# One load of raw inputs split into four pieces, each with a tile of its own

## The chip, the cores and the metric

The kernel runs on one NeuronCore of a Trainium2 chip. The core has five engines with a queue of instructions each: TensorE (PE, matrix products; PEld is its weight loading), VectorE (DVE), ScalarE (ACT), GpSimd (POOL) and SyncE (SP), which in this kernel issues every DMA. Each engine works through its queue in order, and an instruction whose input is not there yet holds up all that stand behind it. The metric is the time of one execution on the device, in microseconds (us); lower is better.

## The reference

Six arrays r, k, v, w, a, b of shape 4 x 8 x 768 x 40 (batch, heads, time steps, features) drive a recurrence with a 40 x 40 state per batch and head. Its output goes through two dense layers with different gates:

```
for t in range(768):                      # for each of 4 x 8 batch-heads
    y[t]  = r[t] @ state
    Sa    = state @ a[t]
    state = state * w[t][None, :] - outer(Sa, b[t]) + outer(v[t], k[t])
x = y as 3072 tokens x 320
h = x @ w_in;   x = (h * sigmoid(h)) @ w_out       # first layer, d_ff 2048
h = x @ w_in2;  out = (h - tanh(h)) @ w_out2       # second layer
```

## The kernel before

The 768 steps are cut into 12 chunks of 64, and each chunk into two halves (`hf`) of 16 batch-heads. In a chunk the recurrence is rewritten as matrix products with running products of w. Work on a chunk c goes through these steps:

- `load_raw` (L196): one DMA brings the half's packed inputs from the DRAM tensor `pk` into the tile `raw`, 120 partitions x 2311 float32: 384 columns of a, 768 of k and b, 384 of r, 384 of v, and 391 of w, in this order. `raw` has one buffer. The second half of chunk 0 is an exception and goes into a spare `LR` buffer.
- `prep` (L210): DVE runs a forward scan over w (L226), a reciprocal (L227), two small writes of `HL` (L228, L229) and a scaling of a (L231), then a backward scan over w (L232) and a scaling of k and b (L235). POOL scales r and v (L194, called at L238) and subtracts (L191, L241) to get the low float16 parts of numbers that ACT rounds to float16 (L236, L237, L239, L240). The result `HL` (one buffer) goes to an `LR` tile (five buffers) in 12 SBUF-to-SBUF DMAs (L252).
- `p1`, `p2`: products of the features (L267, L287), their masked copies `mK` (L275) and `bP` (L279, L280).
- `sol_in`, 31 times `sol_step`, `sol_out`: a triangular solve on DVE (L302, L311, L313, L323, L324), then two merges on PE (L331, L345).
- `ch_x`, `ch_u`, `ch_s`, `ch_y`, `ch_m`: the chain over chunks, mostly PE with short evictions; the state goes on in `MT` and `M`, copied by DMA (L447, L448, L477, L478). The `LR` buffer of a half is free after them. In this stretch DVE also evicts `lows` (L387, L475), `Md` (L437) and `Sm` (L407).
- `x_t1`, `x_t2`, with the decay factors `pf` loaded at L482 and scanned at L487; then the first dense layer for the chunk's 256 tokens: `mm_h` (L567, L568), `act1`, `mm_o` (L589 to L591), `out1`.

Beside these the weights of both layers are converted (`conv_wi`, `conv_wo`: loads of `cr` at L515, work at L523 to L526). The second layer is a stage of its own after everything else.

The table `SC` gives each step of each chunk a time in an abstract unit; the steps are traced in the order of these times, and a scheduler then fixes each engine's order with a model of durations and of buffers that come free. So a change of a tile or a load can move instructions of all engines. For `load_raw` the time is that of `raw`, kept behind the `prep` of the half before.

Of the kernel before, what the change touches and what calls it, by code (L numbers as in the profile page):

```python
# [7 lines left out]
F32 = mybir.dt.float32  # L8
# [10 lines left out]
C = 64  # L19
# [7 lines left out]
RAWN = 5 * 384 + 391  # L27
# [4 lines left out]
S_R = 2.0 ** 10  # L32
# [15 lines left out]
def _poly():  # L48
# [21 lines left out]
    raw=(-10.4107, -10.0452),  # L70
# [13 lines left out]
    x=(-0.5853, 0.3603, 0.8835, 1.3808),  # L84
    xe=0.02,
    u=(0.6994, 1.3329, 1.3307, 2.0705),
# [13 lines left out]
    o=4.7895,  # L100
# [5 lines left out]
def build(tc, pk, tv, wf, w1i, w1o, w2i, w2o, out, nch=NCH, dbg=None):  # L106
    nc = tc.nc
    PE, ACT, DVE, POOL, SP = nc.tensor, nc.scalar, nc.vector, nc.gpsimd, nc.sync
# [13 lines left out]
    at_p = ph1.enter_context(tc.tile_pool(name="at", bufs=1))  # L122
# [56 lines left out]
    def planes(HL):  # L179
        return [HL[:, :, o:o + n] for o, n in ((0, LW), (LW, 2 * C), (RW, LW), (RW + LW, 2 * C))]  # L180
# [5 lines left out]
    P_t, raw_t, L_t, R_t, KBt_t, VU_t, MT_t, M_t, U_t = {}, {}, {}, {}, {}, {}, {}, {}, {}  # L186
# [3 lines left out]
    def psub(out, a, b):  # L190
        POOL.tensor_tensor(out, a, b, ALU.subtract)  # L191

    def pscale(out, a, sc):
        POOL.tensor_scalar(out, a, sc, 0.0, ALU.mult, ALU.add)  # L194

    def load_raw(c, hf):  # L196
        if c == 0 and hf == 1:
            t = lr_slot().rearrange("p u n -> p (u n)").bitcast(F32)[0:120, 0:RAWN]
        else:
            t = at_p.tile([120, RAWN], F32, tag="raw", name="raw", bufs=1)  # L200
        SP.dma_start(out=t, in_=pk[c, hf])
        raw_t[c, hf] = t

    def load_v(c, hf):
        t = VU_s[hf]
# [2 lines left out]
        VU_t[c, hf] = t  # L208

    def prep(c, hf):  # L210
        raw = raw_t.pop((c, hf))
        hl = HL
        if c == 0 and hf == 1:
            hl = lr_slot().rearrange("p u n -> p (u n)")[0:120, 0:12 * RW].rearrange("p (j n) -> p j n", j=6)
            DVE.memset(planes(hl)[0][:, :, 3 * C:LW], 0.0)
        ll, rh, lh, rl = planes(hl)
        k0, v0 = (0, 2 * C) if c % 2 == 0 else (C, 0)

        def sl(i, n):
            return raw[:, i:i + 6 * n].rearrange("p (j t) -> p j t", t=n)  # L220

        av, kb, rv, vv, w = sl(0, C), sl(384, 2 * C), sl(1152, C), sl(1536, C), raw[:, 1920:RAWN]

        pt = at_p.tile([120, 392], F32, tag="pq", name="pq", bufs=1)
        pq = pt[:, 0:390].rearrange("p (j t) -> p j t", t=65)
        DVE.tensor_tensor_scan(pt[:, 0:390], w[:, 0:390], d1a.rearrange("p j t -> p (j t)"), 0.0, ALU.mult, ALU.add)  # L226
        DVE.reciprocal(out=d1b[:, 65:391:65], in_=pt[:, 64:390:65])  # L227
        DVE.tensor_scalar(lh[:, :, 3 * C:3 * C + 1], pq[:, :, C:C + 1], S_P * S_KB / P_INIT, None, ALU.mult)  # L228
        DVE.scalar_tensor_tensor(out=lh[:, :, 3 * C + 1:LW], in0=pq[:, :, C:C + 1], scalar=S_P * S_KB / P_INIT,  # L229
                                 in1=lh[:, :, 3 * C:3 * C + 1], op0=ALU.mult, op1=ALU.subtract)  # L230
        DVE.scalar_tensor_tensor(out=av, in0=av, scalar=-S_A * S_KB, in1=pq[:, :, 0:C], op0=ALU.mult, op1=ALU.mult)  # L231
        DVE.tensor_tensor_scan(pt[:, 2:391][:, ::-1], w[:, 2:391][:, ::-1], d1b[:, 2:391][:, ::-1], 0.0, ALU.mult, ALU.add)  # L232
        pi = pt[:, 2:392].rearrange("p (j t) -> p j t", t=65)[:, :, 0:C]
        kbv = kb.rearrange("p j (q t) -> p j q t", q=2)
        DVE.tensor_tensor(kbv, kbv, pi.unsqueeze(2).to_broadcast([120, 6, 2, C]), ALU.mult)  # L235
        ACT.activation(out=lh[:, :, k0:k0 + 2 * C], in_=kb, func=AF.Copy)  # L236
        ACT.activation(out=rh[:, :, 0:C], in_=av, func=AF.Copy)  # L237
        pscale(raw[:, 1152:1920], raw[:, 1152:1920], S_R)  # L238
        ACT.activation(out=rh[:, :, C:2 * C], in_=rv, func=AF.Copy)  # L239
        ACT.activation(out=lh[:, :, v0:v0 + C], in_=vv, func=AF.Copy)  # L240
        (DVE if c == 0 else POOL).tensor_tensor(ll[:, :, k0:k0 + 2 * C], kb, lh[:, :, k0:k0 + 2 * C], ALU.subtract)  # L241
        psub(rl[:, :, 0:C], av, rh[:, :, 0:C])
        psub(ll[:, :, v0:v0 + C], vv, lh[:, :, v0:v0 + C])
        psub(rl[:, :, C:2 * C], rv, rh[:, :, C:2 * C])
        if c == 0:
            gates["pool"] = nc.cur_bb.bb.instructions[-1]
        LR = lr_slot()
        for i in range(3):
            n = 6 if i < 2 else 4
            src, dst = hl[i * 40:i * 40 + 40, 0:n], LR[:, 6 * i:6 * i + n]  # L250
            for pl, s0, d0, w in ((0, RW, 0, LW), (0, LW, LW, 2 * C), (1, RW, 0, RW), (2, 0, 0, RW)):
                SP.dma_start(out=dst[pl * 40:pl * 40 + 40, :, d0:d0 + w], in_=src[:, :, s0:s0 + w])  # L252
        LR = LR[0:120].rearrange("p (u j) n -> p u j n", u=2)
        L, R = LR[:, :, :, 0:LW], LR[:, :, :, LW:RW]
        if c == 0:
            gates["sp"] = nc.cur_bb.bb.instructions[-1]
        p63 = at_p.tile([40, 2, 8, 1], F32, tag="p63", name="p63", bufs=5)
        POOL.tensor_tensor(p63, L[0:40, :, :, 3 * C:3 * C + 1], L[0:40, :, :, 3 * C + 1:LW], ALU.add)
        L_t[c, hf], R_t[c, hf], P_t[c, hf] = L, R, p63
# [36 lines left out]
    def lr_slot():  # L296
        return at_p.tile([128, 16, RW], F16, tag="LR", name="LR", bufs=5)
# [357 lines left out]
    for c in range(nch):  # L655
        T0 = 8.0 * c
        T1 = T0 + (SC["d"][c] if c < len(SC["d"]) else 0)
        for hf in range(2):
            when(T1 + SC["raw"][hf], load_raw, c, hf, after=[("prep", c - 1 + hf, 1 - hf)] if c else [])
            when(T1 + SC["prep"][hf], prep, c, hf, after=[("load_raw", c, hf)] + ([("prep", c, 0)] if hf else []))  # L660
            when(T0 + SC["v"][hf], load_v, c, hf, after=[("ch_y", c - 1, 2 * hf), ("ch_y", c - 1, 2 * hf + 1)])
# [15 lines left out]
        for nm, fn, fe in (("x", ch_x, ch_xe), ("u", ch_u, ch_ue), ("s", ch_s, ch_se), ("y", ch_y, ch_ye), ("m", ch_m, ch_me)):  # L677
            for b in range(4):
                hf = b // 2
# [25 lines left out]
    if not dbg:  # L705
        for f in range(NF):
            at(SC["c1"][0] + f * SC["c1"][1], conv_w1, conv_wi, mo, w1i, wih[:, f], f)
            at(SC["c1"][0] + SC["c1"][2] + f * SC["c1"][1], conv_w1, conv_wo, mo, w1o, woh[:, f], f)
            for q in range(2):
                n = 2 * f + q  # L710
# [79 lines left out]
```

## Time and profile before

| what | value |
|---|---|
| median of three runs | 1278.87 us (1276.74 to 1279.15) |
| profiled execution | 1283.47 us, of which 1281.4 us are the profile's span |
| mean granted TensorE clock | 0.932 of full speed |
| busy share of the span | PE 83%, DVE 76%, ACT 64%, POOL 33% |
| raw loads | 23 into `raw`, one into `LR`, 1083.3 KB each |

The span begins with a stretch of some 100 us in which PE has almost nothing to do. From there to about 860 us chunks overlap with the first dense layer. What is left of the first layer runs to about 900 us, the second layer's weights are loaded, and the second layer takes the last 351 us. Times in the rows below are us from the start of the span unless they say ns.

### The profile page before, as it was taken

The numbers are of one execution on the slowest core, as the hardware profiler recorded it, in microseconds if no ns is written. First come the engines' busy times: TensorE is split into PE (matmuls) and PEld (weight loads), VectorE is DVE, ScalarE is ACT, GpSimd is POOL, SyncE is SP. The second block draws the span as 40 slices with busy tenths as digits, with TensorE's granted clock in tenths as the row PEclk, the third lists the DMA queues.
The fourth block names the chain that finished last, engine by engine and source line by source line (L and its number), as shares of the span: only waits on it lengthen the run. The fifth ranks groups of instructions, "written<-read, shape, count | busy, mean of one in ns | idle before, by whom it ended". The sixth has DMA issues, their size and how long they took to land.

```text
span 1281.4 us, 31698 instructions
## 1 busy us (share of the span) xinstructions
PE 1063.9 (83%) x12624; PEld 879.2 (69%) x12624; DVE 971.2 (76%) x1871; ACT 822.5 (64%) x1586; POOL 421.6 (33%) x490
## 2 busy tenths in 40 slices
PE   0006578798889889889888998999999999999997
PEld 0005566677677667767776777888778888888885
DVE  6678998788887868878677787853238788888885
ACT  2456687666767657645545454554259888888886
POOL 5334544434424333423232231010013333333332
PEclk9999759879898979989897998999989999999999
DMA  5565665555656554353424432110701111111100
GB/s 129 144 146 154 173 155 138 146 146 147 159 143 171 141 160 114 101 116 96 108 74 96 108 94 74 31 47 21 216 24 24 24 33 27 33 25 24 24 12 21
DMA packets 154955, 122.36 MB, mean 95 GB/s; under 512 B 89528, under 2 KB 140152, under 8 KB 151928
## 3 DMA queue, kind: packets, MB, share of 16 engines
q1 hardware_dynamic: 154808, 120.35, 36.5%
q8 instruction: 99, 1.62, 0.5%
q14 instruction: 48, 0.39, 0.1%
HBM read 63.59 MB, written 13.89 MB: 60 GB/s over the span
## 4 chain that ended last, share of the span: by engine, by line
PE 22%; issue 18%; DMA 17%; DVE 17%; POOL 9%; SPq 8%; ACT 8%; POOLq 0%; DVEq 0%; ACTq 0%
DMA raw<-pk 8%; POOL gl L191 7%; PE hp L567 7%; SPq L252 5%; DMA LR<-HL 3%; DVE Tl L313 3%; DVE tmp L311 2%; PE o L589 2%; PE o L591 2%; PE o L590 2%; DMA pf<-wf 2%; SPq L632 2%; PE psx L361 2%; PE psu L376 1%; ACT cr L525 1%
## 5 line engine op out<-in xcount | busy, mean ns | idle before, releaser
L567 PE MATMUL hp<-xh,wih 128*128 128x256 f16 x960 | 196.7, 291 | 13.9 <-DVE gl L577 13.7
L567 PE MATMUL hp<-x,w 128*128 128x256 f16 x1344 | 189.5, 273 | 0.0
L191 POOL TENSOR_TENSOR gl<-q,gh 128x512 f16<-128x512 f32 x96 | 111.3, 1159 | 207.8 <-ACT gh L624 207.8
L567 PEld LDWEIGHTS <-wih 128*128 128x128 f16 x1344 | 131.9, 103 | 39.5 <-issue 15.4
L567 PEld LDWEIGHTS <-w 128*128 128x128 f16 x1344 | 131.5, 98 | 22.9
L313 DVE TENSOR_TENSOR Tl<-Tl,tmp 128x126 f32<-128x126 f32 (+22 forms) x372 | 130.3, 350 | 7.6
L311 DVE TENSOR_TENSOR tmp<-Al,Tl 128x126 f32<-128x126 f32 (+22 forms) x372 | 120.4, 324 | 8.2 <-ACT Al L303 1.2
L267 PE MATMUL p1a<-LR 120*128 120x64 f16 x384 | 28.5, 207 | 116.7 <-DMA LR<-HL 69.9
L589 PE MATMUL o<-woh,gh 128*128 128x320 f16 x384 | 120.0, 313 | 5.9 <-DVE x2o L600 5.3
L591 PE MATMUL o<-woh,gl 128*128 128x320 f16 x384 | 118.6, 315 | 2.7 <-DVE gl L577 2.7
L590 PE MATMUL o<-woh,gh 128*128 128x320 f16 x384 | 119.7, 312 | 0.0
L590 PE MATMUL o<-w,gh 128*128 128x320 f16 x384 | 112.5, 299 | 0.0
L589 PE MATMUL o<-w,gh 128*128 128x320 f16 x384 | 111.3, 299 | 1.4 <-ACT gh L624 1.3
L567 PE MATMUL hp<-xl,wih 128*128 128x256 f16 x384 | 111.6, 291 | 0.1
L267 PEld LDWEIGHTS <-LR 120*128 120x128 f16 x384 | 21.6, 105 | 123.5 <-issue 108.9
L591 PE MATMUL o<-w,gl 128*128 128x320 f16 x384 | 102.5, 299 | 1.0 <-POOL gl L191 1.0
L590 PEld LDWEIGHTS <-gh 128*128 128x128 f16 x768 | 76.7, 100 | 32.6 <-issue 5.5
L591 PEld LDWEIGHTS <-gl 128*128 128x128 f16 x768 | 76.4, 100 | 31.0 <-DVE gl L577 3.4
L589 PEld LDWEIGHTS <-gh 128*128 128x128 f16 x768 | 76.6, 100 | 30.0 <-ACT gh L624 2.0
L577 DVE SCALAR_TENSOR_TENSOR gl<-hp,gh 128x512 f16<-128x512 f32 x96 | 65.5, 682 | 41.2 <-ACT gh L576 37.8
L619 DVE SCALAR_TENSOR_TENSOR s<-s,z 128x512 f32<-128x512 f32 x96 | 70.7, 737 | 32.9 <-ACT s L617 31.8
L575 ACT ACTIVATE hp<-hp 128x512 f32<-128x512 f32 x96 | 56.2, 587 | 49.0 <-PE hp L568 47.0
(147 smaller groups left out, 2952.1 us busy)
## 6 DMA issues: line engine op xcount, KB each, us to landing
raw<-pk SPq DMA_DIRECT2D x23, 1083.3 KB
LR<-HL SPq DMA_DIRECT2D x92, 150.9 KB
cr<-w1i SPq DMA_DIRECT2D x16, 384.0 KB
cr<-w2i SPq DMA_DIRECT2D x16, 384.0 KB
cr<-w1o SPq DMA_DIRECT2D x16, 320.0 KB
cr<-w2o SPq DMA_DIRECT2D x16, 320.0 KB
w2d<-w2s SPq DMA_DIRECT2D x32, 160.0 KB
w<-w2d SPq DMA_DIRECT2D x4, 1280.0 KB
```

What stands on the lines that cost most here:

```text
L191: POOL.tensor_tensor(out, a, b, ALU.subtract)
L252: SP.dma_start(out=dst[pl * 40:pl * 40 + 40, :, d0:d0 + w], in_=src[:, :, s0:s0 + w])
L267: PE.matmul(pa[:, p, :], kb, R[:, u, p, 0:C], start=True, stop=True)
L311: DVE.tensor_tensor(tv_, Al[:, j + 1:, j:j + 1].to_broadcast([128, n, w]), Tl[:, j:j + 1, :w].to_broadcast([128, n, w]), ALU.mult)
L313: DVE.tensor_tensor(Tl[:, j + 1:, :w], Tl[:, j + 1:, :w], tv_, ALU.add)
L567: PE.matmul(o, wi[:, f, a], x[:, k], start=n == 0, stop=False)
L575: ACT.activation(out=hp, in_=hp, func=AF.Silu, scale=1.0 / (S_X * S_WI))
L577: DVE.scalar_tensor_tensor(out=gl, in0=hp, scalar=S_G, in1=gh, op0=ALU.mult, op1=ALU.subtract)
L589: PE.matmul(o, gh[:, cs], wo[:, f, 0], start=f == 0, stop=False)
L590: PE.matmul(o, gh[:, cs], wo[:, f, 1], start=False, stop=False)
L591: PE.matmul(o, gl[:, cs], wo[:, f, 0], start=False, stop=f == NF - 1)
L619: DVE.scalar_tensor_tensor(out=s, in0=s, scalar=GAMMA, in1=z, op0=ALU.add, op1=ALU.mult)
```

## The change

The one load of a half becomes four, issued in the order w (391 columns), a (384), k and b (768), r and v (768), each into its own tile: `raww` and `rawa` with two buffers, `rawkb` and `rawrv` with one. `prep` takes its operands from these tiles; what it computes is the same. In the second half of chunk 0 the four pieces go to the same columns of the spare buffer.

```diff
     def load_raw(c, hf):
-        if c == 0 and hf == 1:
-            t = lr_slot().rearrange("p u n -> p (u n)").bitcast(F32)[0:120, 0:RAWN]
-        else:
-            t = at_p.tile([120, RAWN], F32, tag="raw", name="raw", bufs=1)
-        SP.dma_start(out=t, in_=pk[c, hf])
-        raw_t[c, hf] = t
+
+        spare = lr_slot().rearrange("p u n -> p (u n)").bitcast(F32)[0:120] if c == 0 and hf == 1 else None
+        raw_t[c, hf] = []
+        for nm, o, n, k in (("w", 1920, 391, 2), ("a", 0, 384, 2), ("kb", 384, 768, 1), ("rv", 1152, 768, 1)):
+            t = spare[:, o:o + n] if spare is not None else at_p.tile([120, n], F32, tag="raw" + nm, name="raw" + nm, bufs=k)
+            SP.dma_start(out=t, in_=pk[c, hf, :, o:o + n])
+            raw_t[c, hf].append(t)
...
     def prep(c, hf):
-        raw = raw_t.pop((c, hf))
+        w, ra, rkb, rrv = raw_t.pop((c, hf))
...
-        def sl(i, n):
-            return raw[:, i:i + 6 * n].rearrange("p (j t) -> p j t", t=n)
-
-        av, kb, rv, vv, w = sl(0, C), sl(384, 2 * C), sl(1152, C), sl(1536, C), raw[:, 1920:RAWN]
+        av, kb, rv, vv = [x.rearrange("p (j t) -> p j t", j=6) for x in (ra, rkb, rrv[:, 0:384], rrv[:, 384:768])]
...
-        pscale(raw[:, 1152:1920], raw[:, 1152:1920], S_R)
+        pscale(rrv, rrv, S_R)
```

The lines behind the change move up by two (L226 of before is L224, L235 is L233). The scheduler orders all five queues anew. The first place to look at is DVE's queue in the second half of a chunk in the middle of the program. `tmp` and `Tl` are the solve, and a scan is printed as SCALAR_TENSOR_TENSOR. Before, the forward scan of the new half stands between steps of the solve, well behind the first half's last scaling:

```order
L311 TENSOR_TENSOR tmp<-Al,Tl 128x115
L313 TENSOR_TENSOR Tl<-Tl,tmp 128x23x5
L226 SCALAR_TENSOR_TENSOR pq<-raw,d1a 120x390
L311 TENSOR_TENSOR tmp<-Al,Tl 128x110
L387 SCALAR_TENSOR_TENSOR lows<-psu,LR 40x512
L275 TENSOR_TENSOR mK_121<-p1a,mask_k 64x512
L227 RECIPROCAL d1b<-pq 120x6
L228 TENSOR_SCALAR HL<-pq 120x6
L231 SCALAR_TENSOR_TENSOR raw<-raw,pq 120x384
```

In the changed kernel the same scan (L224) follows the first half's backward scan (L230) and scaling of k and b (L233) with one instruction between:

```order
L230 SCALAR_TENSOR_TENSOR pq<-raww,d1b 120x389
L233 TENSOR_TENSOR rawkb<-rawkb,pq 120x768
L575 SCALAR_TENSOR_TENSOR gl<-hp,gh 128x512
L224 SCALAR_TENSOR_TENSOR pq<-raww,d1a 120x390
L225 RECIPROCAL d1b<-pq 120x6
L229 SCALAR_TENSOR_TENSOR rawa<-rawa,pq 120x384
```

The scan has moved ahead of nine steps of the solve (18 instructions); the second half's own scaling of k and b, L233, comes 27 instructions behind it. The second place is SP's queue at about the eighth chunk, between the copies of `M` and of the corrected rows of `LR` (before L390, after L388). Before, a half is one row:

```order
L201 DMA raw<-pk 120x2311
L602 DMA x2d<-x2o 128x2x384
L390 DMA LR<-LR 40x16x64
L602 DMA x2d<-x2o 128x2x384
L390 DMA LR<-lows 40x16x64
L201 DMA raw<-pk 120x2311
L390 DMA LR<-LR 40x16x64
L390 DMA LR<-lows 40x16x64
```

In the changed kernel the pieces of two halves mix with the other copies:

```order
L202 DMA rawkb<-pk 120x768
L600 DMA x2d<-x2o 128x2x384
L202 DMA rawa<-pk 120x384
L202 DMA raww<-pk 120x391
L202 DMA rawrv<-pk 120x768
L475 DMA M<-M 40x640
L476 DMA M<-lows 40x640
L202 DMA rawa<-pk 120x384
L202 DMA rawkb<-pk 120x768
```

Where SP issued one load, it issues w and a of a later half, and the k-b and r-v pieces of the half that is next to be prepared.

## Rows read from the trace of the kernel before

**Rows 1.** The page's chain that ended last: share by engine, by line
```profile
PE 22%; issue 18%; DMA 17%; DVE 17%; POOL 9%; SPq 8%; ACT 8%; POOLq 0%; DVEq 0%; ACTq 0%
DMA raw<-pk 8%; POOL gl L191 7%; PE hp L567 7%; SPq L252 5%; DMA LR<-HL 3%; DVE Tl L313 3%; DVE tmp L311 2%; PE o L589 2%; PE o L591 2%; PE o L590 2%; DMA pf<-wf 2%; SPq L632 2%; PE psx L361 2%; PE psu L376 1%; ACT cr L525 1%
```

**Rows 2.** Busy time of each engine in four stretches
```profile
core 0: us, PE busy (x) PEld busy (x) DVE busy (x) ACT busy (x) POOL busy (x), PEclk, DMA share, GB/s
0.00:100.00 100.00, 5.09 (x56) 3.65 (x57) 68.22 (x131) 38.84 (x70) 42.50 (x70) 1.00 0.58 144
590.00:660.00 70.00, 63.47 (x943) 53.75 (x943) 55.27 (x116) 36.43 (x73) 19.77 (x24) 0.95 0.40 97
800.00:930.00 130.00, 125.55 (x1700) 106.12 (x1697) 61.16 (x130) 58.01 (x118) 9.93 (x15) 0.98 0.27 79
930.00:1281.00 351.00, 342.90 (x2811) 275.42 (x2810) 272.66 (x392) 283.95 (x517) 112.59 (x99) 0.99 0.10 24
```

**Rows 3.** The chain in order of time: start us, us, what
```profile
40.37 9.33 DMA raw<-pk
...
242.47 3.22 DMA cr<-w2i
...
632.42 8.39 DMA raw<-pk
...
676.67 3.58 DMA pf<-wf
...
750.59 7.88 DMA raw<-pk
```

**Rows 4.** All that touches tile raw: loads, then who waited (us, times)
```profile
L201 SPq DMA_DIRECT2D raw<-pk x23: 351/509/585, 0.8 to 750.6; - x23
...
  POOL raw L194: 130.5, 20
  DVE pq L226: 44.9, 21
```

**Rows 5.** DVE in order of time, 600 to 668 us; in brackets idle before
```profile
617.63 0.97 DVE L226 TENSOR_TENSOR_SCAN pq<-raw,d1a 120x390 f32<-120x390 f32 x1 [4.03 <-DMA raw<-pk]
...
640.83 0.97 DVE L226 TENSOR_TENSOR_SCAN pq<-raw,d1a 120x390 f32<-120x390 f32 x1 [3.70 <-DMA raw<-pk]
```

**Rows 6.** Waits of DVE, 130 to 860 us: total us, times, longest
```profile
DVE pq L226 <- DMA raw<-pk: 41.2, 17, 4.6
DVE pf L487 <- DMA pf<-wf: 16.9, 9, 2.9
```

**Rows 7.** The scan of pf, line 487, 130 to 860 us: ns min/median/max
```profile
L487 DVE TENSOR_TENSOR_SCAN pf<-pf,d1f x21: 903/957/2256, 171.7 to 853.2; 128x384 f32<-128x384 f32 x21
```

**Rows 8.** SP's queue in order of time, 670 to 690 us
```profile
677.18 3.24 SPq L252 DMA_DIRECT2D LR<-HL  x4
...
682.98 0.49 SPq L201 DMA_DIRECT2D raw<-pk  x1
```

**Rows 9.** All engines in order of time at the start, 0 to 62 us
```profile
7.54 0.06 DVE L182 MEMSET HL<- 120x6 uint32 x1
...
9.31 0.97 DVE L226 TENSOR_TENSOR_SCAN pq<-raw,d1a 120x390 f32<-120x390 f32 x1 [1.71 <-DMA raw<-pk]
...
15.89 1.43 DVE L487 TENSOR_TENSOR_SCAN pf<-pf,d1f 128x384 f32<-128x384 f32 x1 [4.42 <-DMA pf<-wf]
...
46.82 0.21 DVE L311 TENSOR_TENSOR tmp<-Al,Tl 128x31 f32<-128x31 f32 x1 [0.68 <-ACT Al L303]
...
55.76 1.20 DVE L235 TENSOR_TENSOR raw<-raw,pq 120x768 f32<-120x768 f32 x1
```

**Rows 10.** Waits in the first 130 us: total us, times, longest
```profile
PE p1a L267 <- DMA LR<-HL: 58.3, 7, 26.8
...
DVE mK L275 <- PE p1a L267: 14.4, 7, 6.1
```

**Rows 11.** Waits of SP's queue, 130 to 860 us
```profile
SPq L252 <- PE psm L429: 15.4, 5, 6.2
...
SPq L252 <- PE psy L422: 8.3, 1, 8.3
```

## The prediction, made before the changed kernel ran

> **What bounds the kernel now.** I read the chain that ended last first. Its largest single item with a line of its own is the transfer raw<-pk, 8% of the span; the issue of the copies L252 takes another 5% [rows 1]. In order of time the chain holds 13 of these transfers, the first at 40.37 us and the last at 750.59 us; by the share that is about 105 us, 8.1 us each [rows 3]. That is not yet what the loads cost, since beside most of them other engines had work.
>
> So the second view is that of the stretches [rows 2]. In the first 100 us PE works for 5.09 us: a pure latency stage, in which DVE works for 68.22 us. From about 100 to 860 us the stage is mixed: in the 70 us from 590 on PE works 63.47 us and DVE 55.27 us, and neither is full. From 800 us PE is nearly full (125.55 of 130), since matrix products of the first layer are left over. The last 351 us (second layer) hold no raw load. What the change can do lies before 860 us, and it reaches the end only as far as PE gets its work earlier, for the leftover then shortens one for one.
>
> The third view is who waits for raw. POOL's scaling L194 waits 130.5 us in 20 waits, DVE's forward scan L226 44.9 us in 21 [rows 4]. POOL has 19.77 us of work in those 70 us [rows 2], so its wait mostly costs nothing. DVE's does cost: the scan stands amid steps of the solve, and all of them stand still: 4.03 us at 617.63 and 3.70 us at 640.83 [rows 5]. Between 130 and 860 us that is 41.2 us in 17 waits, the largest wait of DVE in that stretch [rows 6].
>
> **What goes.** raw has one buffer, so a half can only be loaded after the last reader of the half before; the load then takes about 8 us and the scan is the first to need it. In the changed kernel the scan needs only w, whose tile has two buffers. By the order of SP's queue w and a of a later half stand among the pieces of the one being prepared, so they are there when the scan is reached. I take all 44.9 us of scan waits as gone; of them 1.71 us is the first scan's, which can now start when the memsets of DVE end at 7.6 us [rows 9].
>
> **What comes in place.** The tile rawkb still has one buffer. Its load waits for the same last reader as before (the subtraction L241), and the scaling L233 waits for it. That wait is new, and behind it on DVE stand the steps of the solve and the evictions of the chain, for which PE and ACT wait, just as behind the scan. Its size is not in the trace. From below it is zero: in the place shown L233 stands 27 instructions behind its own half's forward scan, among steps of the solve. From above it is the full former wait, 41.2/17 = 2.4 us each, on 22 halves: 53 us. The nearest row is pf, also a one-buffer tile loaded anew each time: 16.9 us of waits in 21 scans, 0.8 us each [rows 6, 7]. The k-b piece has 768 of 2311 columns, 360 KB, about the size of a cr load that took 3.22 us on the chain, where raw takes 7.9 to 9.3 [rows 3]. I take 0.8 x 22 = 18 us. DVE's net relief is 44.9 - 18 = 27 us.
>
> **The start.** Chunk 0 gains little: its scan starts 1.7 us earlier, but the second half's scan stands behind the scan of pf, whose transfer ended only at 15.89 us, and is now queued behind two more pieces [rows 9]. Chunk 1 gains more: its w and a come with the first loads, so L224 to L230 run before the first solve step at 46.82 us, and only k and b are issued where raw was, at 40.37 us [rows 3, 9]. With 3.2 to 4.5 us for them L233 ends near 47 us where L235 ended at 56.96. How much of these 9 us survives is unknown. PE waits 58.3 us for LR<-HL in the first 130 us, so earlier halves help; but DVE itself waits only 14.4 us for PE [rows 10] and has its own work. Bounds 0 and 14 us; I take half, 7 us.
>
> **SP.** 24 loads become 96, so SP issues 72 more. The issue of a whole load takes 351 to 585 ns [rows 4]; at some 430 ns (between the lowest and the median) that is 31 us of SP time, 1.3 us per half. It stands directly behind the twelve copies L252, four of which take 3.24 us [rows 8], and ahead of the copies of M, MT and LR rows. SP's queue is on the chain for 8% of the span [rows 1]; Most of the pieces of w and a can be issued when SP is idle. I charge a quarter, 8 us, with bounds 0 and 31.
>
> The bytes moved are the same, and the compute instructions of prep are the same in kind and number; their cost is zero by that. The two further buffers of w and a hold SBUF only.
>
> The Trainium skill, "DMA: Bandwidth & Descriptors", "Rules for kernel authors", speaks against the change: for full bandwidth use at least 1 MiB per DMA and join small transfers. The same page ("Anatomy of one DMA") fits, for another issuing path, 2.0 us fixed plus bytes at 436 GB/s, by which one raw load would take an estimated 4.5 us and four in turn 10.5 us. The trace differs in the first number (7.9 us), so the sum does not use it; by that rule r and v would land some 6 us later than they did, which would show on POOL's L194.
>
> **The sum.** -27 (DVE) - 7 (start) + 8 (SP) = -26 us on the profiled execution's 1283.47 us (span 1281.4 and 2.1 around it): 1257.5 us. The median of the runs, 1278.87, lies 4.6 us under the profiled one, so the forecast is 1253 us. This counts DVE's relief as arriving whole. It could be less, since PE's own work fills nine tenths of the stage, and more, since PE does not wait for DVE's idle time alone.
>
> **The rivals.**
> *The wait moves to k and b.* The model that orders the queues had the scan some 4 us too early on the chip [rows 5]; if it does the same with L233, each of 22 halves waits the former 2.4 us: 53 us for the 44.9 that go, so +8; SP's 8 us come on top, and the start gives nothing: +16, about 1295 us. It decides from a mean wait of 2.0 us per half (44.9/22), or from 1.7 with SP's price counted. For it: kb is loaded at the same point as raw was. Against it: the transfer is well under half as long, and the reciprocal, the writes of HL and the backward scan of the same half stand before L233 in DVE's queue.
> *It was hidden anyway.* The copies L252 wait for a free LR buffer, 15.4 us behind psm and 8.3 behind psy [rows 11], and PE has 63.47 of 70 us of work. Then halves prepared earlier only wait longer, DVE's relief becomes waits for PE, and the start's 7 us and SP's 8 cancel: 1277 to 1281 us. Against it: those LR waits are six among some 20 halves. That w is prefetched in name only would look the same; SP's order speaks against that.
> *The chain itself shortens.* If the 13 transfers on the chain are its true cost, each of about 8.1 us becomes a k-b piece of 3.2 us [rows 3]: 13 x 4.9 = 64 us, 1215 us. Against it: the chain names the last of several waits, and DVE idled at most 4.6 us before a scan [rows 6], so other paths end soon after.
>
> **How the numbers follow.** Forecast (a gain between 8 and 50 us) 0.55; chain shortens 0.12; hidden anyway 0.09, the same as within 0.2%, that is 2.6 us, about what a measurement of this kernel tells from no change; the wait moves 0.20; a small gain of 3 to 8 us 0.04. Faster is 0.55 + 0.12 + 0.04 = 0.71, the same 0.09, slower 0.20. The range leaves about half of the largest gains and a third of the slower case out, 0.06 and 0.07: 1228 to 1290 us. The forecast's own range is 1229 to 1271.
>
> **What would show it.** The scan L224 without idle time before it from the second half on, and raww absent from the chain. If the wait moved: idle before L233, released by DMA rawkb, near 50 us in all. If SP is the price: longer waits for LR<-HL, MT and M copies on PE and POOL at unchanged DVE waits. If hidden: more idle in SP's queue at L250 released by psm and psy, and DVE's busy time per 70 us as it was. At the start, the first L233 of chunk 1 near 47 us, and PE busy in the first 100 us well above 5.09. The forecast is wrong if the stretch up to the last raw load does not shorten, or if PE's granted clock and idle time between 130 and 860 us stay as they are.

## The result, and the profile after

The changed kernel took 1243.01 us (median of four runs, 1238.09 to 1244.95) against 1279.01 us for the kernel before in the same comparison (1276.74 to 1283.79). The ratio is 0.9692, with an interval from 0.9661 to 0.9723: faster by 36 us, where 26 us were forecast. The profiled execution spans 1239.6 us, 41.8 us less than the 1281.4 of before.

The first question is where the 41.8 us lie. The last 391 us of both kernels, as busy times of PE, PEld, DVE, ACT and POOL, then granted clock, DMA share and GB/s; first the kernel before:

```profile
890.00:1281.00 391.00, 379.00 (x3152) 305.28 (x3149) 282.84 (x408) 296.86 (x542) 115.28 (x104) 0.99 0.15 40
```

and the changed kernel:

```profile
849.00:1240.00 391.00, 379.41 (x3129) 305.34 (x3127) 282.80 (x406) 295.85 (x540) 115.14 (x103) 0.99 0.15 40
```

The two stretches agree within 1.1 us on every engine. So the whole difference arises before 849 us, in the stage with raw loads, and nothing of it is given back later. That stage in steps of 210 us, in the kernel before:

```profile
100.00:310.00 210.00, 158.23 (x2121) 136.79 (x2121) 178.76 (x384) 148.42 (x295) 91.10 (x106) 0.84 0.58 149
310.00:520.00 210.00, 185.88 (x2491) 151.81 (x2488) 174.48 (x370) 147.37 (x292) 83.48 (x103) 0.90 0.55 147
520.00:730.00 210.00, 183.37 (x2562) 153.49 (x2563) 160.01 (x355) 106.66 (x219) 62.97 (x75) 0.89 0.41 100
```

and in the changed kernel, with the first 100 us ahead ([rows 2] has that row of before: PE 5.09, DVE 68.22):

```profile
0.00:100.00 100.00, 5.81 (x64) 4.11 (x64) 76.05 (x147) 45.87 (x85) 52.74 (x78) 1.00 0.64 172
100.00:310.00 210.00, 162.84 (x2231) 141.60 (x2232) 183.53 (x385) 151.86 (x305) 86.58 (x112) 0.83 0.55 152
310.00:520.00 210.00, 183.19 (x2603) 153.35 (x2601) 179.28 (x388) 145.86 (x293) 85.51 (x104) 0.95 0.53 147
520.00:730.00 210.00, 196.62 (x2814) 167.76 (x2813) 171.87 (x386) 117.23 (x239) 63.07 (x74) 0.92 0.39 101
```

DVE is busier in every stretch and works through more instructions, and PE gets through more matrix products: 110, 112 and 252 more in the three long ones. The growth is largest in the last. The same shows in the place at which DVE transposes the input of a chunk's solve (`sol_in`), here chunks 1, 2, 3, 6 and 10 of the kernel before (counted from 0):

```profile
109.89 1.94 DVE L302 STREAM_TRANSPOSE Al<-bP 64x1024 f32<-64x1024 f32 x1
...
172.53 1.94 DVE L302 STREAM_TRANSPOSE Al<-bP 64x1024 f32<-64x1024 f32 x1
...
253.99 1.89 DVE L302 STREAM_TRANSPOSE Al<-bP 64x1024 f32<-64x1024 f32 x1
...
466.98 1.95 DVE L302 STREAM_TRANSPOSE Al<-bP 64x1024 f32<-64x1024 f32 x1
...
740.91 1.96 DVE L302 STREAM_TRANSPOSE Al<-bP 64x1024 f32<-64x1024 f32 x1
```

and the same five chunks of the changed kernel:

```profile
103.96 1.93 DVE L300 STREAM_TRANSPOSE Al<-bP 64x1024 f32<-64x1024 f32 x1
...
172.33 1.94 DVE L300 STREAM_TRANSPOSE Al<-bP 64x1024 f32<-64x1024 f32 x1
...
246.15 1.91 DVE L300 STREAM_TRANSPOSE Al<-bP 64x1024 f32<-64x1024 f32 x1
...
453.09 1.94 DVE L300 STREAM_TRANSPOSE Al<-bP 64x1024 f32<-64x1024 f32 x1
...
704.84 1.89 DVE L300 STREAM_TRANSPOSE Al<-bP 64x1024 f32<-64x1024 f32 x1
```

The gain is 5.9 us at chunk 1, 0.2 at chunk 2, 7.8 at chunk 3, 13.9 at chunk 6 and 36.1 at chunk 10. Most of it builds up from chunk to chunk, 4.5 us each in the mean between chunks 2 and 10.

What released DVE? Its waits in the changed kernel over the whole span, total us, times, longest:

```profile
DVE pf L485 <- DMA pf<-wf: 24.7, 16, 3.9
...
DVE rawkb L233 <- DMA rawkb<-pk: 0.5, 1, 0.5
```

and POOL's for the same inputs:

```profile
POOL rawrv L194 <- DMA rawrv<-pk: 16.9, 11, 2.7
POOL rawrv L194 <- DMA raww<-pk: 8.7, 1, 8.7
```

The 44.9 us in 21 waits of the scan [rows 4] are gone, none remains before L224, and the scaling of k and b waits once, for half a microsecond. POOL's 130.5 us became 25.6. The chain that ended last agrees:

```profile
PE 25%; issue 19%; DVE 17%; DMA 12%; POOL 10%; SPq 8%; ACT 7%; POOLq 0%; DVEq 0%; ACTq 0%
POOL gl L191 7%; PE hp L565 7%; SPq L250 5%; DMA LR<-HL 4%; DMA pf<-wf 3%; DVE Tl L311 3%; DVE tmp L309 3%; PE o L587 2%; PE o L589 2%; PE o L588 2%; SPq L630 2%; PE psu L374 2%; PE psy L418 2%; PE psx L359 2%; ACT cr L523 2%
```

Against [rows 1], no raw piece is among the items shown any more (it was the first, 8%), and the share of DMA fell from 17% to 12%.

Some of the relief was spent elsewhere. DVE's other waits between 130 and 820 us of the changed kernel:

```profile
DVE c L524 <- ACT cr L523: 13.2, 17, 2.0
DVE HL L226 <- DMA LR<-HL: 10.5, 4, 4.6
```

These two were 5.5 and 5.0 us between 130 and 860 us of before. SP's copies into `LR` wait for a buffer about as long as before: 24.9 us behind psm, and none behind psy any more, where [rows 11] had 15.4 and 8.3:

```profile
SPq L250 <- PE psm L427: 24.9, 6, 7.3
```

The instructions of `prep` are the same, but some of them take longer. The forward scan takes 1405 ns in the mean where it took 978, the scaling of a 843 where it took 590; other DVE instructions became shorter, and DVE's busy time as a whole went from 971.2 to 967.3 us.

### The profile page after: what moved, and what is told of

It is laid out like the page before. It is cut to its first block, busy times and chain, and to the rows that moved or that the text cites. A ratio compares the mean times of both kernels' runs of the same rounds, so it can differ in the third digit from the quotient of the medians.

```text
span 1239.6 us, 31870 instructions
## 1 busy us (share of the span) xinstructions
PE 1044.1 (84%) x12624; PEld 872.2 (70%) x12624; DVE 967.3 (78%) x1871; ACT 819.0 (66%) x1586; POOL 415.5 (34%) x490
## 4 chain that ended last, share of the span: by engine, by line
PE 25%; issue 19%; DVE 17%; DMA 12%; POOL 10%; SPq 8%; ACT 7%; POOLq 0%; DVEq 0%; ACTq 0%
POOL gl L191 7%; PE hp L565 7%; SPq L250 5%; DMA LR<-HL 4%; DMA pf<-wf 3%; DVE Tl L311 3%; DVE tmp L309 3%; PE o L587 2%; PE o L589 2%; PE o L588 2%; SPq L630 2%; PE psu L374 2%; PE psy L418 2%; PE psx L359 2%; ACT cr L523 2%
## 5 line engine op out<-in xcount | busy, mean ns | idle before, releaser
L565 PE MATMUL hp<-xh,wih 128*128 128x256 f16 x960 | 191.1, 286 | 8.2 <-DVE gl L575 8.1
L311 DVE TENSOR_TENSOR Tl<-Tl,tmp 128x126 f32<-128x126 f32 (+22 forms) x372 | 121.0, 325 | 7.5
L587 PE MATMUL o<-woh,gh 128*128 128x320 f16 x384 | 115.9, 303 | 5.7 <-DVE x2o L598 4.2
L588 PE MATMUL o<-woh,gh 128*128 128x320 f16 x384 | 115.9, 303 | 0.0
L589 PE MATMUL o<-woh,gl 128*128 128x320 f16 x384 | 114.0, 303 | 0.1
L575 DVE SCALAR_TENSOR_TENSOR gl<-hp,gh 128x512 f16<-128x512 f32 x96 | 65.6, 684 | 41.6 <-ACT gh L574 39.1
L621 DVE COPY_PREDICATED q<-mk,t 128x512 f32<-128x512 int32 x96 | 79.6, 829 | 10.1 <-ACT z L613 0.5
```

Source lines behind the costliest of these rows:

```text
L311: DVE.tensor_tensor(Tl[:, j + 1:, :w], Tl[:, j + 1:, :w], tv_, ALU.add)
L565: PE.matmul(o, wi[:, f, a], x[:, k], start=n == 0, stop=False)
L575: DVE.scalar_tensor_tensor(out=gl, in0=hp, scalar=S_G, in1=gh, op0=ALU.mult, op1=ALU.subtract)
L587: PE.matmul(o, gh[:, cs], wo[:, f, 0], start=f == 0, stop=False)
L588: PE.matmul(o, gh[:, cs], wo[:, f, 1], start=False, stop=False)
L589: PE.matmul(o, gl[:, cs], wo[:, f, 0], start=False, stop=f == NF - 1)
```

## The experiments

Each comparison has its own runs of the kernel before. The table gathers all that ran; the waits are those of DVE for any piece of the raw inputs, in the profiled execution of each kernel. The gain is against the median of the kernel before in the same comparison.

| kernel | median us | ratio, interval | gain us | DVE's raw waits us | relief us |
|---|---|---|---|---|---|
| before | 1279.01 | 1 | 0 | 44.9 | 0 |
| changed | 1243.01 | 0.9692, 0.9661 to 0.9723 | 36.0 | 0.5 | 44.4 |
| e1 four DMAs, one tile | 1246.87 | 0.9720, 0.9661 to 0.9780 | 35.5 | 4.4 | 40.5 |
| e2 four tiles, one buffer each | 1249.04 | 0.9746, 0.9698 to 0.9795 | 33.3 | 12.1 | 32.8 |
| e3 w apart, rest whole | 1299.32 | 1.0135, 1.0093 to 1.0176 | -17.0 | 42.0 | 2.9 |
| e4 k and b with two buffers | 1262.26 | 0.9842, 0.9797 to 0.9887 | 20.1 | 10.0 | 34.9 |
| e5 one tile, w last | 1250.42 | 0.9770, 0.9735 to 0.9805 | 28.7 | 14.8 | 30.1 |
| e6 eight pieces | 1251.62 | 0.9768, 0.9730 to 0.9806 | 27.5 | 3.2 | 41.7 |
| e7 changed, w last | 1240.93 | 0.9692, 0.9655 to 0.9730 | 38.2 | 7.3 | 37.6 |
| e8 before, other order | 1305.34 | 1.0202, 1.0162 to 1.0241 | -26.2 | 44.2 | 0.7 |
| e9 before, scans later | 1288.47 | 1.0070, 1.0047 to 1.0093 | -8.8 | 37.8 | 7.1 |
| e10 a one buffer, pf two | 1255.01 | 0.9818, 0.9777 to 0.9860 | 24.7 | 3.4 | 41.5 |
| e11 e1 with pf two | 1245.04 | 0.9749, 0.9707 to 0.9791 | 34.7 | 7.4 | 37.5 |
| e12 e7, a one buffer, pf two | 1243.44 | 0.9727, 0.9682 to 0.9772 | 36.3 | 6.0 | 38.9 |

The first four take the change apart. **e1** keeps the one tile with its one buffer and only cuts the DMA:

```diff
-        SP.dma_start(out=t, in_=pk[c, hf])
+        for o, n in ((1920, 391), (0, 384), (384, 768), (1152, 768)):
+            SP.dma_start(out=t[:, o:o + n], in_=pk[c, hf, :, o:o + n])
```

> The load of before, into the one tile with its one buffer, issued as four DMAs in the order w, a, k-b, r-v. Own buffers (what gains is that w's tile comes free early and is loaded again while the rest of the half is still prepared): no piece can start before the last reader of the half before, so the scan still waits, only for some 3.3 us of w in place of 8; scan waits of 15 to 45 us stay, and the time is 1260 to 1280 us. Granularity (what gains is that a needed piece lands sooner, whatever its buffer): 1240 to 1250 us, the scan's waits near zero. Order (any new order of the queues of this size would move the time as much): anywhere from 1240 to 1300 us, without a link to the scan's waits.

It came out 35.5 us faster, with an interval that covers the changed kernel's ratio: tiles and second buffers are not needed for nearly all of the gain. So the one buffer was not the whole cause. In the kernel before it set the time of the load only in some halves. The second half of chunk 8 and the first half of chunk 9, each with the last reader of the half before it (POOL, L241) and SP's issue of the load:

```profile
538.19 1.55 POOL L241 TENSOR_TENSOR HL<-raw,HL 120x768 f16<-120x768 f32 x1
...
551.59 0.52 SPq L201 DMA_DIRECT2D raw<-pk  x1
...
559.59 0.97 DVE L226 TENSOR_TENSOR_SCAN pq<-raw,d1a 120x390 f32<-120x390 f32 x1 [4.57 <-DMA raw<-pk]
...
567.73 1.54 POOL L241 TENSOR_TENSOR HL<-raw,HL 120x768 f16<-120x768 f32 x1 [1.98 <-ACT HL L236]
...
569.30 0.37 SPq L201 DMA_DIRECT2D raw<-pk  x1
```

The second of these loads goes out 0.03 us after the buffer is free. The first goes out 11.85 us after, and in between SP issues other copies almost without a pause. From chunk 3 on all loads of a chunk's second half were issued 6 us or more after the buffer was free; their scans hold 22.9 of the 40.6 us of scan waits there. In each of these nine gaps SP spent three quarters or more of the time issuing other DMAs, above all the copies of the half just prepared into `LR` (L252). The loads of a first half, from chunk 4 on, came 0 to 2.1 us after it was free.

How one buffer can do in e1 shows in one half, SP's issues and DVE's scan (here L227) in order of time:

```profile
550.05 0.83 SPq L202 DMA_DIRECT2D raw<-pk  x2
...
552.51 1.16 SPq L202 DMA_DIRECT2D raw<-pk  x2
552.76 0.97 DVE L227 TENSOR_TENSOR_SCAN pq<-raw,d1a 120x390 f32<-120x390 f32 x1 [0.16 <-DMA raw<-pk]
```

The last reader of the half before ends at 549.68; w is issued at 550.05 and the scan runs 2.71 us later, waiting 0.16. The piece of w (about 180 KB) is there well before a whole load would be: where a scan waited in e1 its w had been issued 2.7 to 3.9 us earlier, where one waited in the kernel before, from chunk 3 on, the whole load had been issued 7.5 to 8.8 us earlier (8.03 at 617.63). DVE's waits for the tile:

```profile
DVE pq L227 <- DMA raw<-pk: 4.2, 6, 1.1
```

**e2** gives the four tiles of the changed kernel one buffer each, **e4** gives the second buffer to k and b instead of w and a:

```diff
-        for nm, o, n, k in (("w", 1920, 391, 2), ("a", 0, 384, 2), ("kb", 384, 768, 1), ("rv", 1152, 768, 1)):
+        for nm, o, n, k in (("w", 1920, 391, 1), ("a", 0, 384, 1), ("kb", 384, 768, 1), ("rv", 1152, 768, 1)):   # e2
+        for nm, o, n, k in (("w", 1920, 391, 1), ("a", 0, 384, 1), ("kb", 384, 768, 2), ("rv", 1152, 768, 1)):   # e4
```

> Four tiles and four DMAs as in the changed kernel, but one buffer each. Own buffers: w's tile is free after the backward scan, before the last scaling, the rounding and the subtractions, so w is loaded beside them; scan waits of 0 to 15 us, 1243 to 1255 us. If the second buffer itself is what counts: scan waits above 30 us and 1265 us or more. Granularity: 1240 to 1250 us.

> Four tiles, but the second buffer goes to k-b in place of w and a (the same space within 28 bytes). Own buffers: like the kernel with one buffer each, 1243 to 1255 us, since nothing waited long for k-b. If the remaining one-buffer load of k-b is the next bound: below 1240 us.

e2 gains 33.3 us, within what was expected for waits of 0 to 15 us. e4 came out slower than both of its expected ranges: it has as much relief as e2 (34.9 and 32.8 us) and yet gains 13 us less. Its raw waits don't explain that, and the cause stays open; the scheduler's other order is a guess that no run isolates.

**e3** keeps w's second buffer and loads the other 1920 columns whole into one tile with one buffer:

```diff
-        for nm, o, n, k in (("w", 1920, 391, 2), ("a", 0, 384, 2), ("kb", 384, 768, 1), ("rv", 1152, 768, 1)):
+        for nm, o, n, k in (("w", 1920, 391, 2), ("r", 0, 1920, 1)):
...
-        w, ra, rkb, rrv = raw_t.pop((c, hf))
+        w, rr = raw_t.pop((c, hf))
+        ra, rkb, rrv = rr[:, 0:384], rr[:, 384:1152], rr[:, 1152:1920]
```

> Two tiles: w (two buffers) and one tile of 1920 columns for a, k, b, r and v (one buffer), so 48 loads in place of 96. Own buffers of w alone: the scan's waits are gone and SP issues 48 loads less, 1238 to 1248 us. Granularity: the scaling of a and of k and b waits for a load of 900 KB, some 7 us, behind the last reader; waits of 30 us or more on DVE before the scaling of a or of k-b, and 1255 to 1270 us.

It is 17 us slower than the kernel before, outside both of its expected ranges. The scan no longer waits, and the scaling of a (L230) does, in DVE's waits and in one half:

```profile
DVE rawr L230 <- DMA rawr<-pk: 41.6, 21, 4.3
```

```profile
632.31 0.56 DVE L230 SCALAR_TENSOR_TENSOR rawr<-rawr,pq 120x384 f32<-120x384 f32 x1 [3.02 <-DMA rawr<-pk]
```

This is the rival of the moved wait, come true in a neighbour of the changed kernel: 41.6 us in 21 waits in place of 44.9 in 21. To free only the first reader is worth nothing here. It is not that the second reader stands close behind the first: where L230 waited, at least 13 other DVE instructions and 9 us lay between the scan and it. But its load of 900 KB had been issued only 6.7 to 9.0 us before L230 ran. Nearly equal waits explain why nothing is gained; they don't explain the 17 us that are lost, and no run does.

Is it the order of the pieces, then? **e5** is e1 with w last, **e7** the changed kernel with w last, and **e6** the changed kernel with each piece cut once more:

```diff
+        for o, n in ((1152, 768), (384, 768), (0, 384), (1920, 391)):   # e5
...
+        for nm, o, n, k in (("rv", 1152, 768, 1), ("kb", 384, 768, 1), ("a", 0, 384, 2), ("w", 1920, 391, 2)):   # e7
...
+            for q0, q1 in ((0, n // 2), (n // 2, n)):   # e6, around the load of each piece
+                SP.dma_start(out=t[:, q0:q1], in_=pk[c, hf, :, o + q0:o + q1])
```

> As the four DMAs into one tile with one buffer, in the reverse order: r-v, k-b, a, w. If what counts is that the piece the scan needs lands first: w now lands last, some 8 us after the buffer is free, the scan waits 40 us or more in all, and the time is 1275 to 1300 us. If four small DMAs are simply faster than one large, whatever their order: scan waits below 15 us and 1243 to 1255 us.

> The changed kernel with the order of issue reversed: r-v, k-b, a, w, the second buffers of w and a kept. Own buffers: the second buffer of w makes its place among the four unimportant; scan waits below 8 us, 1243 to 1255 us. Order of landing: the scan waits 20 us or more and 1260 us or more.

> The changed kernel with each of its four pieces loaded in two DMAs of half its columns, so SP issues 96 loads more. If SP's issue time has the price of the prediction (8 us for 72 issues): 11 us more, 1254 us. If SP has room: 1238 to 1249 us, and no wait of another engine for raw pieces grows.

e7 is as fast as the changed kernel: with w last but two buffers for it, no scan waits. What DVE waits for is small and comes from the pieces that have one buffer:

```profile
DVE rawkb L233 <- DMA rawkb<-pk: 5.0, 3, 2.1
...
DVE HL L226 <- DMA rawrv<-pk: 2.3, 1, 2.3
```

e5 has neither: one buffer, and w last. Its scans do wait, 14.8 us in 12 waits, here one of them with SP's issue of the four pieces:

```profile
DVE pq L227 <- DMA raw<-pk: 14.8, 12, 3.0
```

```profile
613.04 2.33 SPq L202 DMA_DIRECT2D raw<-pk  x4
...
620.08 0.97 DVE L227 TENSOR_TENSOR_SCAN pq<-raw,d1a 120x390 f32<-120x390 f32 x1 [1.51 <-DMA raw<-pk]
```

This scan ran 7.04 us after the first issue. Over the 12 that waited it is 7.9 us in the mean (6.9 to 8.9), against 8.0 for the 16 from chunk 3 on that waited for the whole load: the four pieces together are as late as the whole. What differs is when DVE comes to the scan: 6.6 us after the issue in the mean (in the one shown 7.04 less 1.51, that is 5.53), where it came after 5.5 before, and eleven scans needn't wait at all. The issue stands earlier in relation to the scan. The pieces' columns do not come free one after the other: in e1 and e5 no piece of a half was issued before the last reader of the half before had ended. What is left is the place that the scheduler gives to the scan when it has four loads to place; no run isolates that. So with w last and no second buffer splitting still buys 28.7 us, and neither w's early arrival nor its second buffer is the reason there. Time and waits came out in the range expected if four small DMAs were simply faster than one large, but the pieces were there no sooner.

e6 doubles SP's issues once more (96 more than the changed kernel). DVE's raw waits grow by only 2.7 us, the time by 8.6 us between medians and by 0.76% between ratios, 9.7 us. By the prediction's price for SP (8 us for 72 issues) 96 cost 11. That agrees, but the order changed with it too, so it is no clean measurement.

**e8** was meant to ask how much the order alone can do. It is the kernel before with the products `p2` placed 0.4 units later in the table `SC`.

```diff
-    p2=(1.1248, 1.2019, 1.4012, 1.5709),
+    p2=(1.5248, 1.6019, 1.8012, 1.9709),
```

> The kernel of before with the times of p2 and its eviction put 0.4 units later (p2 is off the loads' path); the scheduler then orders about as many instructions of DVE anew (939 rows of difference, against 1118 by the change itself). Order alone: the time moves by 15 to 40 us either way while the scan's waits for raw stay near 45 us. Loads: 1265 to 1295 us with the scan's waits at 35 to 55 us.

It is 26 us slower at nearly unchanged scan waits (44.2 us in 23):

```profile
DVE pq L226 <- DMA raw<-pk: 44.2, 23, 4.0
```

But it is no test of the order alone. The step `ch_u` is traced behind `p2`, so the first `ch_u` of a chunk (L376) moved behind the chunk's fourth `ch_x`. The four quarters of a chunk share three tiles `Xs`, so the fourth quarter's `Xs` now overwrites the first quarter's before that is read: e8 leaves out the first quarter's own values, and its first products wait for the fourth quarter. In the kernel before, two `ch_u` run ahead of the fourth `Xs`:

```profile
550.91 1.09 PE L376 MATMUL psu<-TT,Xs 128*40 128x64 f32 x16
...
562.95 0.42 ACT L368 ACTIVATE Xs<-psx 64x320 f32<-64x320 f32 x1
```

In e8, from chunk 1 on, all four `Xs` stand ahead of the first:

```profile
582.28 0.42 ACT L368 ACTIVATE Xs<-psx 64x320 f32<-64x320 f32 x1
...
582.75 1.93 PE L376 MATMUL psu<-TT,Xs 128*40 128x64 f32 x16 [4.69 <-ACT Xs L368]
```

So the chain over the chunks has a new dependency, and the 26 us can be its price. How far order alone moves this kernel was not measured. The nearest figures are those of kernels that compute the same: e2 and e4 differ by 13 us, and e3 and the kernel before by 17 us, each pair at nearly equal raw waits.

**e9** asks the reverse: the kernel before, with the scans of 15 halves held back behind named steps of the solve, some two to nine steps later than they stood, and nothing else.

```diff
+        with ExitStack() as st:
+            if 2 * c + hf in late:
+                st.enter_context(tc.issue_after(steps[late[2 * c + hf]]))
             DVE.tensor_tensor_scan(pt[:, 0:390], w[:, 0:390], d1a.rearrange("p j t -> p (j t)"), 0.0, ALU.mult, ALU.add)
```

> The kernel of before, with its one load and one buffer; only the forward scan of 15 halves whose scan waited (0.9 to 4.6 us each) is held in DVE's queue behind a later step of the solve (some 2 to 9 steps). If the cost is the place of the scan in DVE's queue, since the queue's model took the large load for shorter than it is: scan waits below 15 us in all and 1240 to 1260 us, without any change of the load. If the load itself must land sooner: 1270 to 1290 us, for each half is prepared as late as before.

It is 0.7% slower. The waits became fewer but longer, 37.8 us in 14:

```profile
DVE pq L231 <- DMA raw<-pk: 37.8, 14, 6.0
```

The load moved with the scan where that could be seen best. In the half with the longest wait the last reader of the half before (L246) was done at 593.75, and SP, issuing other copies meanwhile, came to the load 9.1 us later:

```profile
592.20 1.55 POOL L246 TENSOR_TENSOR HL<-raw,HL 120x768 f16<-120x768 f32 x1 [0.21 <-ACT HL L241]
...
602.86 0.46 SPq L203 DMA_DIRECT2D raw<-pk  x1
...
612.16 0.97 DVE L231 TENSOR_TENSOR_SCAN pq<-raw,d1a 120x390 f32<-120x390 f32 x1 [6.01 <-DMA raw<-pk]
```

So setting the scan later, at these places, does not do what an early piece does. It does not exclude better places.

The last three ask for more: if a DVE wait for a one-buffer tile costs its length, a second buffer for pf should bring its waits back as well. **e10** is the changed kernel with one buffer for a and two for pf, **e11** e1 with two for pf, **e12** e7 with one for a and two for pf.

```diff
-        t = at_p.tile([128, 3, 128], F32, tag="pf", name="pf", bufs=1)
+        t = at_p.tile([128, 3, 128], F32, tag="pf", name="pf", bufs=2)
```

> The changed kernel with the second buffer of a given to pf (the decay factors of the output), whose scan waits 24.7 us for its load in the changed kernel. If each us of DVE standing still for a load counts, as with raw: pf's waits below 8 us and 1218 to 1230 us. If only raw's place in the chain counted: 1236 to 1250 us at the same fall of pf's waits.

> Four DMAs into one tile with one buffer, w first, and two buffers for pf. DVE's waits for loads: raw's 4 us as without the second buffer of pf, pf's below 8 from 26.7; if they count one for one, 1225 to 1235 us, else 1240 to 1252.

> The changed kernel with the pieces issued in the order r-v, k-b, a, w, one buffer for a, two for w and two for pf. As the kernel with w first: 1215 to 1230 us if DVE's waits for pf count one for one, 1236 to 1250 us if not.

None is faster than its neighbour. The waits of the scan of pf fell in all three: from 24.7 us (changed) to 12.7 in e10 and from 25.6 (e7) to 20.1 in e12; below 8 was expected of e10 and e11. In e11 they fell from 26.7 us (e1) to:

```profile
DVE pf L488 <- DMA pf<-wf: 15.5, 9, 4.8
```

and the time stayed within the intervals (0.9749 beside 0.9720). So here a second buffer ended only part of the waits; what holds the other loads was not followed. And the 5 to 12 us of DVE's waits for pf that went bought no time that shows: a microsecond of DVE's waits is not always worth a microsecond. e10 lost 11 us against the changed kernel and lies outside both of its expected ranges; e12, with the same edit, lost 2 against e7. No version beats the changed kernel by more than its interval.

## Why the prediction was right, and where its sizes were off

**What bounds the kernel: right.** The wait of the scan in DVE's queue was a cost that the change could win back. Across the table, the ten kernels with under 15 us of DVE waits for raw pieces, the changed one among them, are 20 to 38 us faster than before, and the three that kept 37.8 us or more are 9 to 26 us slower. Gain and relief are not equal: gain less relief lies between -20 and +1 us without e8, whose chain differs. So the sign goes with the wait in every kernel. Every one of them also has another order; that ten orders with short waits are all faster, and e3 and e9 with long waits slower, speaks against order as the reason for the gain, but its share in the size stays open. No single difference under some 15 us between two of these kernels can be put down to the wait.

**What goes: right in size, half right in cause.** All 44.9 us went. The prediction said that raw's one buffer holds the load back and that w's second buffer frees it. From chunk 4 on the buffer held the load back in the first halves of chunks; in the second halves the load came 6 us or more after the buffer was free, since SP was still issuing copies that stood ahead of it. And e1 and e2 show that w's second buffer is not needed: with one buffer w comes first, about 3 us after its issue in e1; with two it may come last (e7). e5, with neither, still has 30.1 us of relief, from scans that stand later after the issue. The changed kernel has both; between it and e2, which lacks the buffers, lie 2.7 us of gain, within the intervals.

**What comes in place: this is the step that was mis-sized.** The prediction put 0.8 us on each of 22 halves before L233, 18 us, between bounds of 0 and 53. It measured 0.5 us in one wait: the lower bound. Of the two arguments that stood against the rival, that the piece is short is the one that the runs bear out. In the changed kernel the load of k and b was issued as little as 4.1 us before L233, without a wait; where e3's load of 900 KB was waited for, it took 6.7 to 9.0 us. That instructions stand ahead of the reader did not save e3. e2, with one buffer for k and b as in the changed kernel, had 0.8 us there. Where the second load is long, as in e3, the rival's price is real.

**The start: right at first, its end open.** Locally the step came as worked out, and sooner. The changed kernel's DVE at the start:

```profile
7.51 0.96 DVE L224 TENSOR_TENSOR_SCAN pq<-raww,d1a 120x390 f32<-120x390 f32 x1
...
15.22 1.51 DVE L485 TENSOR_TENSOR_SCAN pf<-pf,d1f 128x384 f32<-128x384 f32 x1 [3.85 <-DMA pf<-wf]
...
42.65 0.96 DVE L233 TENSOR_TENSOR rawkb<-rawkb,pq 120x768 f32<-120x768 f32 x1 [0.45 <-DMA rawkb<-pk]
```

The first scan starts 1.8 us earlier, the scan of pf 0.7, and chunk 1's scaling of k and b runs at 42.65 and ends at 43.61, where an end near 47 was expected and L235 began only at 55.76 before [rows 9]. Chunk 1's solve starts 5.9 us earlier. But chunk 2's starts only 0.2 us earlier and chunk 3's 7.8, so how much of the start's gain reached the end can't be read off, and PE's work in the first 100 us rose from 5.09 to 5.81 us, not "well above".

**SP: not shown.** The prediction's sign was longer waits for the copies on PE and POOL. In the first 130 us PE's wait for the copies into `LR` grew from 58.3 us [rows 10] to 67.1:

```profile
PE p1a L265 <- DMA LR<-HL: 67.1, 7, 23.1
```

Yet in the kernel before the same products also waited once for a load of weights, and that wait is gone from the changed kernel:

```profile
PE p1a L267 <- DMA cr<-w1i: 24.1, 1, 24.1
```

All waits of these products together fell in that stretch, from 99.7 to 84.8 us, and POOL's for the copies (at L258 of before, L256 of changed) fell over the whole span from 81.6 to 67.9. e6's 9 us for 96 further issues fit 8 for 72, with the reservation above.

DVE's net relief came out at 44 us where the prediction had 27. With the forecast's own 8 us for SP and nothing for the start the sum is -44 + 8 = -36 us, which is the measured gain. But neither of these two terms was measured by itself, so agreement this close is partly chance.

**Whether DVE's relief reaches the end: yes.** The prediction left open that PE's nine tenths might swallow it. Of the 41.8 us by which the span fell, PE's idle time gave 22.0 (217.5 to 195.5) and its busy time 19.8 (1063.9 to 1044.1) at the same 12,624 products, at a mean granted clock, over its two levels of 1.2 and 2.4 GHz, of 0.945 of full speed in place of 0.932. Busy time times clock is 991.6 and 986.7 us, so the shorter busy time is nearly all clock. Which comes first, fewer stalls or a higher clock, no run here separates: over the profiled kernels of the table the clock mostly goes with the time, from 0.917 in e3 to 0.953 in e7, though e1 has 0.937 at about the changed kernel's time.

**The rivals.** "The wait moves" is refuted for the change and realised in e3. "It was hidden anyway" falls with the gain itself; its sign, more waiting of SP for psm and psy, is 24.9 us where 23.7 stood before. "The chain itself shortens" gave 64 us and is too much: the measured gain is 36, and the copies into `LR` (3% to 4%) and the loads of pf (2% to 3%) took part of the raw loads' place on the chain.

**The rule on transfers.** POOL's L194 waited 25.6 us after the change and 130.5 before. The Trainium skill, "DMA: Bandwidth & Descriptors", "Rules for kernel authors", advises at least 1 MiB per DMA for full bandwidth and joining small transfers; by an estimate from "Anatomy of one DMA" in the same page, given there for another issuing path, r and v were to land some 6 us later. The runs disagree for this kernel: r and v's reader waited less, and in e5, where w comes last of the four, the scan that waited for it ran 7.9 us after the first issue in the mean, where the whole load took 8.0.

## What to carry to other kernels

When an in-order engine waits for a load into a single buffer, look first at how much of the load its next instruction needs: the same bytes in several DMAs, in the order of their use, recovered nearly as much here as tiles with second buffers, without the memory. Check with the end of the last reader and the time of issue whether the buffer holds the load back at all; here it was in half of the cases the queue of the engine that issues the loads. Follow the wait to the second reader before you count it as gone (e3), and judge the new wait by the time from the issue of its load to that reader against the length of the load, not by the nearest wait of the same kind. Where a scheduler orders all queues anew, kernels with nearly equal waits can lie 13 to 17 us apart (e2 and e4, e3 and before), so test an explanation on several kernels that share the suspected cause rather than on one. And when a control moves a step, check that it still reads the same data (e8 did not).

## What the runs showed of the hardware that was not expected

A whole load of 1083 KB took 7.5 to 8.8 us from its issue until the waiting scan ran (from chunk 3 on in the kernel before; earlier ones took 8.0 to 11.1). Its piece of w, some 180 KB, took 2.7 to 3.9 us when it was issued first (e1), and the same piece issued as the last of four was there 6.9 to 8.9 us after the first issue (e5). So four DMAs behind each other cost no more here than one of the same bytes, and the first sixth of the bytes was there in about 40% of the time (3.2 us in the mean against 8.0). What sets the 8 us was not measured by itself.
